# Value sums added by VectorE out of PSUM, both heads' maxima closed together, seven banks in plain rotation

## The chip, the cores and the metric

The kernel runs on one core of one Trainium2 chip. The metric is device time in microseconds, the median of several executions. TensorE (PE, with its weight loads shown as PEld), VectorE (DVE), ScalarE (ACT), GpSimd (POOL) and SyncE (SP, which here only issues transfers) each work through their own list of instructions in order and wait for each other by semaphores. TensorE writes its products into PSUM, which has eight banks of 128 partitions x 512 fp32 numbers; DVE and ACT read them there.

## The reference

The output mixes two branches over the same input x (2048 tokens, 512 features) by a gate for each token:

```python
g = _sigmoid((x * gate_w).sum(-1, keepdims=True))
a = _A_ref(x, A_wqkv, A_wo)
b = _B_ref(x, B_w_gate, B_w_up, B_w_down)
return g * a + (1 - g) * b

# _A_ref: softmax attention, 32 heads of 16, then @ wo
scores = jnp.einsum("bhqd,bhkd->bhqk", q, k) * scale
p = _softmax(scores, axis=-1)
o = jnp.einsum("bhqk,bhkd->bhqd", p, v)

# _B_ref: gated unit with hidden size 1792
h = _sigmoid(x @ w_gate) * (x @ w_up)
return h @ w_down
```

All is fp32. The softmax is taken with the row maximum subtracted, so for each head and query the maximum over 2048 keys has to be known before the exp.

## The kernel before

**Setup (to about 90 us).** The first projections and v are computed, and the maxima of the first queries.

**Main loop.** 16 pairs of heads, 16 steps for each, 256 steps k in all (`NPER`). The two heads of a pair live in the two row halves of TensorE: head b uses partitions 64b and up. One step does five kinds of work, in an order that is written out by hand:

- *Score products* (`st_part`, L638): keys x queries of a pair, 128 keys x 512 queries each, eight a step; ACT turns each into p by an exp (L640). A fifth group of rows of the query tile `QS` carries the negative maximum of that query, so the product is already shifted. In even steps all eight are of head 0 (`t0`), in odd steps of head 1 (`t1`): four for this step and four for the next.
- *Maximum products* (`sm_step`, L298): queries x keys without the shift, eight steps (head 0) or ten (head 1) ahead of their use; DVE reduces each to a maximum per query (L300) in a tile `stat`. They are `m0` and `m1` in the order.
- *Half products* (`dense`, `d0` and `d1`): twelve a step, of half the rows each, into the bank `dn`; they are the remaining q and k projections (L152) and the gated unit's products (L172). When a sum is done, ACT copies it out (`leave`, L573), and POOL combines it further through a list of jobs, `later`, of which `work(n)` runs n.
- *The value product* (`values(k)`, L779) at the end of a step: p times v of four blocks of keys for both heads, 32 weight loads and products with all rows of TensorE, into one bank. Four steps make a sum. ACT copies the first of the four into `sum` and the others into `part` (L784); POOL adds `part` to `sum` (L797) as the first job of `later`, and after the fourth SP stores it (`pv_d`). In the last eight steps (`TAIL`) DVE makes these copies (L786).
- *Closing maxima* (`close_max`): a block is 512 queries of one head. When its sixteen reduces are done, DVE takes the maximum of four (L312), POOL splits it into two parts in the next step (L102, L103), DVE turns it from columns into rows (L322) two steps after the closing, and SP sends it into `QS` by four small transfers (L328). The heads are closed apart: head 1's block two steps ahead of head 0's.

**What sets the order.** The order on each engine is that of the program. `STEADY` names the products of an even and of an odd step for the first 248 steps, `LAST` those of the last eight. `place` gives out banks: seven banks circulate (`seven`), and by `REUSE` a product takes the bank that was given out six, seven or eight places earlier, so 17 places make a step (eight t, eight m, one value product). A product waits until the engine that reads the bank's last content is through with it. `urgent` holds what the next step does at the word `work`.

**After the loop (from about 1490 us)** the hidden layer's down product and the heads' output product run, almost all on TensorE.

Of the kernel before, what the change touches and what calls it, by code (L numbers as in the profile page):

```python
# [25 lines left out]
P = 128  # L26
# [9 lines left out]
FIRST = 16  # L36
# [14 lines left out]
def gated_mix(ctx, tc, x, xc, xmix, wqk, wv, wo, w_gu, w_down, gate_w, out):  # L51
# [214 lines left out]
    square = turns([(mxs[:, i, 40:44].bitcast(F32), mxs[:, i, :40]) for i in range(2)])  # L266
# [18 lines left out]
    def sm_step(j):  # L285
# [5 lines left out]
        def one(b, i):  # L291
            part = (p, qt // 4, b)
            if part not in stat:
                stat[part] = keep.tile([P, 4, 4], F32, name=f"stat{p}_{qt // 4}_{b}", tag="stat", bufs=8)
                count[part] = 0
# [4 lines left out]
            dve.tensor_reduce(stat[part][:, qt % 4, g:g + 1], t, axis=AX.X, op=ALU.max)  # L300
            count[part] += 1
            if count[part] == 16:
                full.append(part)
# [4 lines left out]
    def close_max():  # L308
        part = full.pop(0)
        p, i, b = part  # L310
        m, hl = square()
        dve.tensor_reduce(m, stat.pop(part), axis=AX.X, op=ALU.max)  # L312
        two = hl[:, :8].rearrange("p (t c) -> p t c", c=2)
# [4 lines left out]
        def turned():  # L318
            f = hl.bitcast(F32)
            blocks = bass.AP(f.tensor, f.offset, [f.ap[0], (2, 4), (1, 32)])  # L320
            mt = keep.tile([P, 4, 32], F32, name=f"mt{p}_{i}_{b}", tag="mt", bufs=2)
            dve.transpose(mt, blocks)  # L322

            def send():
                r = 64 * b + 3 * DH
                rows = QS[p % 2][r:r + 2, i * 512:(i + 1) * 512].bitcast(F32).rearrange("a (t g j) -> a g t j", g=4, j=32)
                for g in range(4):
                    sp.dma_start(rows[:, g], mt[32 * g:32 * g + 2])  # L328
# [348 lines left out]
    bank7 = turns(seven)  # L677
# [91 lines left out]
    def values(k):  # L769
# [12 lines left out]
        def copy(e):  # L782
            if k < NPER - TAIL:
                act.activation(e, o, AF.Copy)  # L784
            else:
                dve.tensor_copy(e, o)  # L786

        if part not in sums:
            sums[part] = keep.tile([P, 256], F32, name=f"sum{p}_{c}", tag="sum", bufs=2)
            copy(sums[part])  # L790
        else:
            e = keep.tile([P, 256], F32, name=f"part{k}", tag="part", bufs=2)
            copy(e)
            later.insert(0, lambda s=sums[part]: add(s, e))

        def add(s, e):
            pool.tensor_tensor(s, s, e, ALU.add)  # L797
            if k % 4 == 3:
                sp.dma_start(pv_d[c, p], s)
# [17 lines left out]
    count_given = [0]  # L817

    def place():
        b = given[-REUSE[count_given[0] % len(REUSE)]]  # L820
        count_given[0] += 1
        given.append(b)
        return b
# [32 lines left out]
    for k in range(NPER):  # L856
        n = 2 * k
        if n + FIRST == NSTEP:
            bank = bank7
# [206 lines left out]
```

## Time and profile before

| | |
|---|---|
| median of 3 runs | 1679.14 us (1679.1 to 1679.32) |
| span of the profiled execution (no other time of it is listed) | 1677.7 us |
| TensorE clock granted | 1.000 |
| busy: DVE, ACT, POOL | 1430.2, 1338.9, 1053.4 us |
| L300 reduces out of `sm` and `st` banks | 1124 and 924, 682 ns each |
| L640 exps out of `sm` and `st` banks | 1217 and 831, 625 and 628 ns each |
| L784 copies on ACT | 248, 385 ns each |
| L797 sums on POOL | 192, 737 ns each |
| L322 transposes, L312 closing maxima on DVE | 128 each, 302 and 128 ns |

How to read the rows: in a timeline each row is the start in us, the length, the engine, the line, the operation, what it writes and reads (out<-in, buffer numbers left out), the form, and how many like instructions were merged; in brackets stands the idle time of the engine in front of it and what ended it. Products are pipelined, so that PE seems always busy; PEld, the weight loads, shows better when PE waits. A group's row gives count, busy time in all, and the mean length.

### The profile page before, as it was taken

The page shows a single profiled execution, that of the slowest core. Times are in us where ns is not written, and L with a number is a line of the kernel's source. Part 1 is how long each engine was busy: PE and PEld are TensorE (multiplying, and loading weights), DVE is VectorE, ACT ScalarE, POOL GpSimd, SP SyncE. Part 2 cuts the span into 40 slices and gives each one's busy share as a digit, 9 for nine tenths or more (in the row PEclk, how much of TensorE's full clock was granted, in tenths as well). Part 3 has the DMA queues.
Part 4 walks back from the last instruction along what each step waited for, and adds up shares of the span by engine and source line. Part 5 has one row for each costly group of instructions (what it writes and reads, how often), then busy time and mean ns, then how long its engine had stood idle before and what let it go on. Part 6 is the DMA issues. An engine that isn't in the chain of part 4 may idle for free.

```text
span 1677.7 us, 43606 instructions
## 1 busy us (share of the span) xinstructions
PE 1672.6 (100%) x16594; PEld 1148.7 (68%) x16594; DVE 1430.2 (85%) x2456; ACT 1338.9 (80%) x2680; POOL 1053.4 (63%) x1238
## 2 busy tenths in 40 slices
PE   9999999999999999999999999999999999999999
PEld 7866666666666666666666666666666666678887
DVE  6989998999999999999999999999999999668653
ACT  4188888888888888888888999999999988974421
POOL 1146665368888888776676897777777767752110
PEclk9999999999999999999999999999999999999999
DMA  9624666454444444442347353423343425268860
GB/s 257 133 80 171 176 206 191 136 152 144 118 149 133 127 140 129 126 118 72 94 151 209 121 138 106 118 92 95 102 100 93 110 79 183 70 226 298 276 198 25
DMA packets 131554, 236.68 MB, mean 141 GB/s; under 512 B 19409, under 2 KB 39889, under 8 KB 128337
## 3 DMA queue, kind: packets, MB, share of 16 engines
q1 hardware_dynamic: 131056, 233.37, 47.1%
q8 instruction: 131, 2.15, 0.6%
q14 instruction: 79, 0.64, 0.1%
q10 hardware_dynamic: 288, 0.52, 0.1%
HBM read 155.71 MB, written 77.59 MB: 139 GB/s over the span
## 4 chain that ended last, share of the span: by engine, by line
PE 99%; DVE 0%; ACT 0%; issue 0%; POOL 0%; ACTq 0%
PE dn L172 23%; PE sm L779 22%; PE sm L298 10%; PE st L298 9%; PE st L779 8%; PE dn L152 7%; PE sm L1002 6%; PE sm L638 4%; PE st L139 4%; PE st L638 3%; PE dn L1002 2%; PE st L152 1%; PE st L1002 1%; PE st L87 0%; ACT p L640 0%; DVE stat L300 0%
## 5 line engine op out<-in xcount | busy, mean ns | idle before, releaser
L300 DVE TENSOR_REDUCE stat<-sm 128x1 f32<-128x512 f32 x1124 | 727.9, 682 | 73.7 <-PE sm L298 30.4
L640 ACT ACTIVATE p<-sm 128x512 f32<-128x512 f32 x1217 | 682.2, 625 | 7.5 <-PE sm L638 5.3
L300 DVE TENSOR_REDUCE stat<-st 128x1 f32<-128x512 f32 x924 | 606.7, 682 | 63.2 <-PE sm L638 24.2
L640 ACT ACTIVATE p<-st 128x512 f32<-128x512 f32 x831 | 495.0, 628 | 1.6 <-PE dn L152 0.2
L172 PE MATMUL dn<-xm,mh 64*128 64x512 f32 x1568 | 485.5, 389 | 0.0
L638 PE MATMUL sm<-qs,ks 64*128 64x512 f32 x1217 | 445.1, 403 | 0.0
L298 PE MATMUL sm<-ks,qs 48*128 48x512 f32 x1124 | 420.8, 421 | 0.1
L298 PE MATMUL st<-ks,qs 48*128 48x512 f32 x924 | 368.0, 426 | 0.0
L779 PE MATMUL sm<-p,v 128*17 128x256 f32 x6080 | 365.2, 380 | 0.1
L638 PE MATMUL st<-qs,ks 64*128 64x512 f32 x831 | 324.7, 408 | 0.0
L172 PEld LDWEIGHTS dn<-xm,mh 64*128 64x128 f32 x1568 | 289.5, 185 | 29.3
L172 PE MATMUL dn<-xm,ml 64*128 64x512 f32 x784 | 304.2, 388 | 0.0
L779 PEld LDWEIGHTS sm<-p,v 128*17 128x17 f32 x6080 | 160.4, 97 | 169.4 <-ACT p L640 58.5
L298 PEld LDWEIGHTS sm<-ks,qs 48*128 48x128 f32 x1124 | 199.9, 184 | 87.4 <-DVE stat L300 77.0
L638 PEld LDWEIGHTS sm<-qs,ks 64*128 64x128 f32 x1217 | 219.0, 185 | 16.0 <-issue 2.1
L298 PEld LDWEIGHTS st<-ks,qs 48*128 48x128 f32 x924 | 167.1, 184 | 83.6 <-DVE stat L300 75.5
L797 POOL TENSOR_TENSOR sum<-sum,part 128x256 f32<-128x256 f32 x192 | 141.5, 737 | 77.7 <-ACT part L784 49.5
L423 POOL TENSOR_TENSOR m<-m,m 128x512 f32<-128x512 f32 x140 | 178.1, 1290 | 5.9 <-ACT m L573 3.9
L638 PEld LDWEIGHTS st<-qs,ks 64*128 64x128 f32 x831 | 152.4, 185 | 11.6 <-issue 1.3
L172 PEld LDWEIGHTS dn<-xm,ml 64*128 64x128 f32 x784 | 144.4, 184 | 11.5
L102 POOL CAST mxs<-mxs 128x4 fp32r<-128x4 f32 x128 | 24.1, 188 | 201.2 <-DVE mxs L312 200.8
L125 POOL TENSOR_TENSOR ml<-r,mh 128x512 fp32r<-128x512 f32 x112 | 143.9, 1285 | 7.0
(313 smaller groups left out, 2351.1 us busy)
## 6 DMA issues: line engine op xcount, KB each, us to landing
r<-in_w_gu_dram SPq DMA_DIRECT2D x112, 256.0 KB
gul<-gu_d SPq DMA_DIRECT2D x56, 512.0 KB
gu_d<-m SPq DMA_DIRECT2D x84, 256.0 KB
xm_d<-xm SPq DMA_DIRECT2D x32, 512.0 KB
xm<-xm_d SPq DMA_DIRECT2D x32, 512.0 KB
xm<-in_xmix_dram SPq DMA_DIRECT2D x24, 512.0 KB
qs<-q_d SPq DMA_DIRECT2D x90, 128.0 KB
ks<-k_d SPq DMA_DIRECT2D x90, 128.0 KB
```

The costliest lines, as they stand in the source:

```text
L125: pool.tensor_tensor(l, src, h.bitcast(F32), ALU.subtract)
L139: pe.matmul(o, a, b, start=(i == 0), stop=(i == len(ops) - 1))
L152: mm = pe.matmul(self.o, a[rows], b[rows], start=(self.n == 0), stop=(self.n == 2 * len(self.ops) - 1))
L172: pe.matmul(self.o, a, b, start=(self.n == 0), stop=(self.n == len(self.ops) - 1))
L298: pe.matmul(t, qs[r:r + KM, qt * P:(qt + 1) * P], ks[r:r + KM, g * 512:(g + 1) * 512], start=True, stop=True)
L300: dve.tensor_reduce(stat[part][:, qt % 4, g:g + 1], t, axis=AX.X, op=ALU.max)
L423: pool.tensor_tensor(o, x, y, op)
L638: pe.matmul(o, ks[r:r + KR, (kt + a) * P:(kt + a + 1) * P], qs[r:r + KR, c * 512:(c + 1) * 512], start=True, stop=True)
L640: act.activation(pt[:, a, :], o, AF.Exp, scale=DH ** -0.5)
L779: pe.matmul(o[r:r + VW, :], v[:, 4 * k % 16 + a, h * VW:(h + 1) * VW], pts[b][:, a, 256 * i:256 * i + 256], start=(a == 0), stop=(a == 3))
L797: pool.tensor_tensor(s, s, e, ALU.add)
L1002: pe.matmul(down[t], a, b, start=(f == 0 and m == 0), stop=(f == NF - 2 and m == 5))
```

## The change

It has four parts.

- `values`: DVE does what ACT and POOL did with the value product. The first of four is copied from PSUM to `sum` by DVE, the other three are added to `sum` by DVE straight from PSUM. `part` and POOL's sums are gone; the store goes through `urgent`. `work` runs one job less at the end of three of four steps, since the sum no longer takes a place in the list.
- `close_max`: a `stat` tile holds both heads; it is closed after 32 reduces by one L312, one split and one L322, and SP sends eight transfers, head 1's first.
- Banks: `REUSE` and its start are gone; `place` goes round the seven banks.
- `STEADY`: another order of the same words, `work` among them.

```diff
--- before.py
+++ after.py
@@ -263,7 +263,7 @@
 
     act.activation(g1[:, :1], warm, AF.Exp)
     mxs = keep.tile([P, 2, 64], F32R, name="mxs")
-    square = turns([(mxs[:, i, 40:44].bitcast(F32), mxs[:, i, :40]) for i in range(2)])
+    square = turns([(mxs[:, i, 48:56].bitcast(F32), mxs[:, i, :48]) for i in range(2)])
     pool.memset(mxs.bitcast(F32), 0.0)
     ones = v.rearrange("p t (h c) -> p t h c", c=VW)[:, :, :, DH]
     pool.memset(ones, 1.0)
@@ -289,17 +289,17 @@
         qs, ks = QS[p % 2], KS[p % 2]
 
         def one(b, i):
-            part = (p, qt // 4, b)
+            part = (p, qt // 4)
             if part not in stat:
-                stat[part] = keep.tile([P, 4, 4], F32, name=f"stat{p}_{qt // 4}_{b}", tag="stat", bufs=8)
+                stat[part] = keep.tile([P, 4, 2, 4], F32, name=f"stat{p}_{qt // 4}", tag="stat", bufs=4)
                 count[part] = 0
             r, g = 64 * b, 2 * kh + i
             t = bankm()
             pe.matmul(t, qs[r:r + KM, qt * P:(qt + 1) * P], ks[r:r + KM, g * 512:(g + 1) * 512],
                       start=True, stop=True)
-            dve.tensor_reduce(stat[part][:, qt % 4, g:g + 1], t, axis=AX.X, op=ALU.max)
+            dve.tensor_reduce(stat[part][:, qt % 4, b, g:g + 1], t, axis=AX.X, op=ALU.max)
             count[part] += 1
-            if count[part] == 16:
+            if count[part] == 32:
                 full.append(part)
         return one
 
@@ -307,25 +307,26 @@
 
     def close_max():
         part = full.pop(0)
-        p, i, b = part
+        p, i = part
         m, hl = square()
-        dve.tensor_reduce(m, stat.pop(part), axis=AX.X, op=ALU.max)
-        two = hl[:, :8].rearrange("p (t c) -> p t c", c=2)
+        dve.tensor_reduce(m, stat.pop(part).rearrange("p t b g -> p (t b) g"), axis=AX.X, op=ALU.max)
+        two = hl[:, :16].rearrange("p (u c) -> p u c", c=2)
 
         def halves():
             split(two[:, :, 0], two[:, :, 1], m, pool, pool)
 
         def turned():
             f = hl.bitcast(F32)
-            blocks = bass.AP(f.tensor, f.offset, [f.ap[0], (2, 4), (1, 32)])
-            mt = keep.tile([P, 4, 32], F32, name=f"mt{p}_{i}_{b}", tag="mt", bufs=2)
+            blocks = bass.AP(f.tensor, f.offset, [f.ap[0], (4, 4), (1, 32)])
+            mt = keep.tile([P, 4, 32], F32, name=f"mt{p}_{i}", tag="mt", bufs=2)
             dve.transpose(mt, blocks)
 
             def send():
-                r = 64 * b + 3 * DH
-                rows = QS[p % 2][r:r + 2, i * 512:(i + 1) * 512].bitcast(F32).rearrange("a (t g j) -> a g t j", g=4, j=32)
-                for g in range(4):
-                    sp.dma_start(rows[:, g], mt[32 * g:32 * g + 2])
+                for b in (1, 0):
+                    r = 64 * b + 3 * DH
+                    rows = QS[p % 2][r:r + 2, i * 512:(i + 1) * 512].bitcast(F32).rearrange("a (t g j) -> a g t j", g=4, j=32)
+                    for g in range(4):
+                        sp.dma_start(rows[:, g], mt[32 * g + 2 * b:32 * g + 2 * b + 2])
             return send
         return halves, turned
 
@@ -674,7 +675,6 @@
     for _, turned in closed:
         turned()()
     seven = [maxb[0], maxb[1], banks[2], maxb[2], banks[1], maxb[3], banks[0]]
-    bank7 = turns(seven)
     chunks = [(c, f) for c in range(NC) for f in range(0, NF, 2)]
 
     def hidden_load(c, f):
@@ -779,24 +779,17 @@
                     pe.matmul(o[r:r + VW, :], v[:, 4 * k % 16 + a, h * VW:(h + 1) * VW],
                               pts[b][:, a, 256 * i:256 * i + 256], start=(a == 0), stop=(a == 3))
 
-        def copy(e):
-            if k < NPER - TAIL:
-                act.activation(e, o, AF.Copy)
-            else:
-                dve.tensor_copy(e, o)
-
         if part not in sums:
             sums[part] = keep.tile([P, 256], F32, name=f"sum{p}_{c}", tag="sum", bufs=2)
-            copy(sums[part])
+            dve.tensor_copy(sums[part], o)
         else:
-            e = keep.tile([P, 256], F32, name=f"part{k}", tag="part", bufs=2)
-            copy(e)
-            later.insert(0, lambda s=sums[part]: add(s, e))
-
-        def add(s, e):
-            pool.tensor_tensor(s, s, e, ALU.add)
-            if k % 4 == 3:
-                sp.dma_start(pv_d[c, p], s)
+            dve.tensor_tensor(sums[part], o, sums[part], ALU.add)
+        if k % 4 == 3:
+            store = lambda s=sums[part]: sp.dma_start(pv_d[c, p], s)
+            if k < NPER - 1:
+                urgent.append(store)
+            else:
+                store()
 
     def mx(b):
         for j in range(UPPER if b else FIRST, NSTEP):
@@ -814,13 +807,7 @@
             yield
 
     urgent = []
-    count_given = [0]
-
-    def place():
-        b = given[-REUSE[count_given[0] % len(REUSE)]]
-        count_given[0] += 1
-        given.append(b)
-        return b
+    place = turns(seven)
 
     def emit(order, **parts):
 
@@ -836,14 +823,8 @@
                 if next(parts[word], place) is place:
                     place()
 
-    STEADY = ("m1 t0 t0 d1 d1 m0 t0 d1 d1 m0 m0 d1 d1 t0 work d1 t0 t0 d1 t0 d1 d1 m0 d1 t0 d1 m0 m0 m1",
-              "m0 t1 t1 d0 m1 d0 t1 d0 d0 m1 t1 d0 d0 m1 work d0 t1 d0 m1 t1 d0 t1 d0 t1 d0 d0 m1 m1 m0")
-    REUSE = (8, 7, 6, 8, 7, 7, 7, 6, 8, 7, 7, 7, 7, 6, 8, 7, 7,
-             6, 8, 6, 8, 7, 7, 7, 6, 8, 7, 7, 7, 7, 7, 7, 7, 6)
-    given = [*range(99)]
-    for j in range(20 * len(REUSE)):
-        given.append(given[-REUSE[j % len(REUSE)]])
-    given = [seven[sorted(set(given[-20:])).index(b)] for b in given[-20:]]
+    STEADY = ("t0 m1 t0 d1 d1 m0 d1 t0 m0 d1 d1 t0 t0 d1 work d1 d1 m0 t0 d1 m0 t0 d1 t0 d1 d1 m0 m1 m0",
+              "m0 t1 d0 t1 m1 d0 d0 t1 d0 d0 t1 d0 m1 d0 work m1 t1 d0 t1 m1 d0 t1 d0 t1 d0 m1 d0 m0 m1")
     LAST = ["t0 d1 t0 d1 t0 d1 t0 d1 d1 work t1 t1 t1 t1", "t0 d1 t0 d1 t0 d1 t0 d1 work t1 t1 t1 t1"] * 2 + [
         "t0 t0 t0 t0 work t1 d0 t1 d0 t1 d0 t1 d0 d0", "t0 t0 t0 t0 work t1 d0 t1 d0 t1 d0 t1 d0"] * 2
 
@@ -855,8 +836,6 @@
     ahead_h = []
     for k in range(NPER):
         n = 2 * k
-        if n + FIRST == NSTEP:
-            bank = bank7
         if 320 <= n < 448 and n % 16 == 0:
             logit_load((n - 320) // 8)
         if n % 32 == 0 and n // 32 + 1 < NPAIR:
@@ -890,7 +869,7 @@
             next(ahead_h[-1])
         if n in (308, 312, 316, 320):
             next(ahead_h[(n - 308) // 4])
-        work(3 if isinstance(run, Sum) and k % 2 else 4)
+        work((3 if isinstance(run, Sum) and k % 2 else 4) - bool(k % 4))
         urgent.extend(jobs)
         if 320 <= n < 448:
             t = (n - 320) // 16 * 2
@@ -986,7 +965,7 @@
     heads = {}
     for n, (c, f) in enumerate(chunks):
         if f == 0:
-            down = [bankt() if 4 * c + t != AHEAD else None for t in range(4)] if c else [maxb[3], banks[0], maxb[0], maxb[1]]
+            down = [bankt() if 4 * c + t != AHEAD else None for t in range(4)] if c else [maxb[0], maxb[1], banks[2], maxb[2]]
         if n == 4:
             g = g0[:, AHEAD:AHEAD + 1]
             dve.tensor_scalar(ahead, dn, g, None, op0=ALU.mult)
```

The rows that follow are the engines' lists as the programs give them, from the middle of the loop (steps 130 and 131); `st` and `sm` with a number are the seven banks, `x2` two alike. Lines past L314 of the changed program are shifted by one or more: L639 there is L638 here, and L329 is L328.

TensorE before, from the last rows of the value product of step 129 into the even step 130:

```order
L779 MATMUL sm_72<-p_1_11202,v 17x256 x2
L779 MATMUL sm_72<-p_0_11149,v 17x256 x2
L298 MATMUL sm_70<-ks_102,qs_101 128x512
L638 MATMUL st_65<-qs_101,ks_102 128x512
L638 MATMUL sm_71<-qs_101,ks_102 128x512
L172 MATMUL dn<-xm_2_4373,mh_0_5_1_10933 128x512 x2
L298 MATMUL sm_69<-ks_102,qs_101 128x512
```

The same place now:

```order
L779 MATMUL st_66<-p_1_10801,v 17x256 x2
L779 MATMUL st_66<-p_0_10740,v 17x256 x2
L639 MATMUL sm_72<-qs_101,ks_102 128x512
L298 MATMUL st_65<-ks_102,qs_101 128x512
L639 MATMUL sm_69<-qs_101,ks_102 128x512
L172 MATMUL dn<-xm_2_4231,mh_0_5_1_10543 128x512 x2
L298 MATMUL sm_70<-ks_102,qs_101 128x512
```

In the even step a score product is now the first and the maximum product the second; the odd step begins with a maximum product in both programs.

TensorE before, at the end of the odd step 131, from its sixth score product to the value product:

```order
L638 MATMUL st_66<-qs_101,ks_102 128x512
L172 MATMUL dn<-xm_3_4685,ml_0_5_1_11091 128x512
L638 MATMUL sm_72<-qs_101,ks_102 128x512
L172 MATMUL dn<-xm_3_4685,mh_0_5_1_11090 128x512
L638 MATMUL sm_70<-qs_101,ks_102 128x512
L172 MATMUL dn<-xm_3_4685,mh_0_5_1_11090 128x512
L172 MATMUL dn<-xm_3_4685,ml_0_5_1_11091 128x512
L298 MATMUL sm_71<-ks_102,qs_101 128x512
L298 MATMUL sm_69<-ks_102,qs_101 128x512
L298 MATMUL st_67<-ks_102,qs_101 128x512
L779 MATMUL st_66<-p_1_11358,v 17x256 x2
```

The same place now:

```order
L639 MATMUL sm_71<-qs_101,ks_102 128x512
L298 MATMUL st_66<-ks_102,qs_101 128x512
L172 MATMUL dn<-xm_3_4531,ml_0_5_1_10697 128x512
L639 MATMUL sm_72<-qs_101,ks_102 128x512
L172 MATMUL dn<-xm_3_4531,mh_0_5_1_10696 128x512
L639 MATMUL st_65<-qs_101,ks_102 128x512
L172 MATMUL dn<-xm_3_4531,mh_0_5_1_10696 128x512
L298 MATMUL sm_69<-ks_102,qs_101 128x512
L172 MATMUL dn<-xm_3_4531,ml_0_5_1_10697 128x512
L298 MATMUL sm_70<-ks_102,qs_101 128x512
L298 MATMUL st_67<-ks_102,qs_101 128x512
L779 MATMUL sm_71<-p_1_10955,v 17x256 x2
```

In both the value product takes the bank of the sixth score product of its step (`st_66` before, `sm_71` now), which is seven places back; two maximum products moved ahead of half and score products, and the three at the end are no longer together.

DVE before, where a step ends and the next begins, in one of the steps with a transpose:

```order
L300 TENSOR_REDUCE stat_2_1_10963<-st_67 128x1
L300 TENSOR_REDUCE stat_2_0_11125<-st_66 128x1
L322 STREAM_TRANSPOSE mt_1_0_11246<-mxs 128x128
L312 TENSOR_REDUCE mxs<-stat_2_1_10963 128x4
L300 TENSOR_REDUCE stat_3_1_11279<-sm_70 128x1
```

The same place now:

```order
L300 TENSOR_REDUCE stat_2_10574<-sm_72 128x1
L300 TENSOR_REDUCE stat_2_10574<-sm_70 128x1
L300 TENSOR_REDUCE stat_2_10574<-st_67 128x1
L300 TENSOR_REDUCE stat_2_10574<-sm_71 128x1
L322 STREAM_TRANSPOSE mt_1_10845<-mxs 128x128
L786 TENSOR_TENSOR sum_0_10795<-st_66,sum_0_10795 128x256
L300 TENSOR_REDUCE stat_3_10878<-st_65 128x1
```

Between the last reduce of a step and the first of the next there now stands the sum of the value product (L786; L784 in one step of four, where it is a copy). L322 is there in one step of four, as before in one of two, and L312 is in another step of the four.

## The prediction

> **What bounds the kernel now.** I read the page first, then the timeline of neighbouring steps. A step k is one pass of the main loop: eight score products (L638) with their exps (L640), eight maximum products (L298) with their reduces (L300), twelve half products into dn, then the value product (L779).
>
> ```profile
> span 1677.7 us, 43606 instructions
> PE 1672.6 (100%) x16594; PEld 1148.7 (68%) x16594; DVE 1430.2 (85%) x2456; ACT 1338.9 (80%) x2680; POOL 1053.4 (63%) x1238
> ```
>
> The span is 1.4 us under the runs' median of 1679.14, so what I save in the span I take off the median. The 100% of PE counts pipelined products and tells nothing of its idle time; DVE (85% of the span) and ACT (80%) are both near it, so each could set the step. Which one does is read from one step, and the timeline shows steps like it all through the main loop:
>
> ```profile
> 807.64 1.43 PEld L779 LDWEIGHTS sm<-p,v 128*17 128x17 f32 x32 [0.31 <-ACT p L640]
> 808.11 1.28 DVE L300 TENSOR_REDUCE stat<-sm 128x1 f32<-128x512 f32 x2
> 808.38 0.68 ACT L573 ACTIVATE m<-dn 128x512 f32<-128x512 f32 x1
> 809.50 0.50 PE L298 MATMUL st<-ks,qs 48*128 48x512 f32 x1
> 809.50 0.50 PE L638 MATMUL sm<-qs,ks 64*128 64x512 f32 x1
> 809.69 0.39 ACT L784 ACTIVATE part<-sm 128x256 f32<-128x256 f32 x1 [0.63 <-PE sm L779]
> 810.03 1.29 DVE L300 TENSOR_REDUCE stat<-st 128x1 f32<-128x512 f32 x2 [0.64 <-PE sm L638]
> ...
> 810.56 0.59 ACT L640 ACTIVATE p<-st 128x512 f32<-128x512 f32 x1
> 811.04 1.09 ACT L640 ACTIVATE p<-sm 128x512 f32<-128x512 f32 x2
> 811.99 1.12 ACT L640 ACTIVATE p<-st 128x512 f32<-128x512 f32 x2
> ...
> 813.16 1.43 PEld L779 LDWEIGHTS st<-p,v 128*17 128x17 f32 x32 [0.31 <-ACT p L640]
> ```
>
> The step takes 813.16 - 807.64 = 5.52 us and is a ring of three pieces. From the value product to the first exp, which starts at 810.06 (row further down): 2.42. From the first exp to the sixth: one distance of 0.50 and four of 0.48, 2.41. The sixth exp ends at 811.99 + 1.12 = 813.11, and 0.05 later the value product begins: it takes the bank that this exp has just read. 2.42 + 2.41 + 0.64 + 0.05 = 5.52. ACT is the limit inside the ring, PE waits 0.31 for it. DVE is not: its eighth reduce ends at 808.11 + 1.28 = 809.39 and the next starts at 810.03, when the new maximum product is there: 0.64 idle in each step.
>
> **Is ACT's value copy in the ring?** In time it stands there, at 809.69, ahead of the first exp. But the first exp comes right behind the end of its own product:
>
> ```profile
> 803.98 0.50 PE L298 MATMUL sm<-ks,qs 48*128 48x512 f32 x1
> 803.98 0.49 PE L638 MATMUL st<-qs,ks 64*128 64x512 f32 x1
> 804.55 0.60 ACT L640 ACTIVATE p<-st 128x512 f32<-128x512 f32 x1
> ...
> 810.06 0.60 ACT L640 ACTIVATE p<-sm 128x512 f32<-128x512 f32 x1
> ...
> 1442.08 1.43 PEld L779 LDWEIGHTS sm<-p,v 128*17 128x17 f32 x32 [0.31 <-ACT p L640]
> 1443.94 0.49 PE L638 MATMUL sm<-qs,ks 64*128 64x512 f32 x1
> 1443.94 0.49 PE L152 MATMUL dn<-wd8h,hh 64*128 64x512 f32 x1
> 1444.13 0.39 ACT L784 ACTIVATE part<-sm 128x256 f32<-128x256 f32 x1 [0.61 <-PE sm L779]
> 1444.46 0.60 ACT L640 ACTIVATE p<-sm 128x512 f32<-128x512 f32 x1
> 1447.56 1.43 PEld L779 LDWEIGHTS sm<-p,v 128*17 128x17 f32 x32 [0.51 <-ACT p L640]
> ```
>
> In the even step the score product ends at 804.47 and the exp starts 0.08 later; in the odd one at 810.00 and 0.06 later. In the last rows no maximum product stands ahead of the score product (a half product in the middle of its sum shares the round and nobody waits for it): exp 0.03 after the end, with the same copy ahead of it, and the step is 1447.56 - 1442.08 = 5.48. So 0.03 to 0.05 of the first exp's wait belongs to the maximum product that is issued and reported first. The copy does not hold the exp: it starts 0.37 ahead of it in the odd step, but only 0.33 ahead at 1444.13, so 0.37 isn't needed. It costs something only where it is itself late:
>
> ```profile
> 211.20 1.43 PEld L779 LDWEIGHTS sm<-p,v 128*17 128x17 f32 x32 [0.31 <-ACT p L640]
> 213.53 0.39 ACT L784 ACTIVATE part<-sm 128x256 f32<-128x256 f32 x1 [1.40 <-PE sm L779]
> 213.81 0.59 ACT L640 ACTIVATE p<-sm 128x512 f32<-128x512 f32 x1
> 216.90 1.43 PEld L779 LDWEIGHTS st<-p,v 128*17 128x17 f32 x32 [0.30 <-ACT p L640]
> ...
>   POOL qh L253: 0.9, 1
>   POOL ha L465: 0.6, 1
>   POOL mh L129: 0.6, 1
> ```
>
> Here it came 2.33 behind the value product's start instead of 2.05, waiting for POOL to give back a buffer; the step took 5.70. (The exp follows after 0.28 even.) The last three rows are L784's waits for POOL: three in all.
>
> **The change, part by part.** *Copies and sums.* Off ACT go 248 copies and off POOL 192 sums; neither stands in the ring, except the three late copies: 3 x (5.70 - 5.52) = **-0.5 us**. DVE gets one operation per step, queued between the eighth reduce and the next step's first. Its price before is not shown (PSUM plus SBUF, 128x256); the neighbours are
>
> ```profile
> 24.53 0.69 DVE L241 TENSOR_TENSOR qe<-st,qe 128x512 fp32r<-128x512 f32 x1 [1.74 <-ACT qe L240]
> ...
> 1467.33 0.42 DVE L786 COPY part<-sm 128x256 f32<-128x256 f32 x1 [2.31 <-PE sm L779]
> 1467.67 0.68 DVE L726 SCALAR_TENSOR_TENSOR gul<-gul 128x512 f32<-128x512 f32 x1
> ...
> 803.79 0.30 DVE L322 STREAM_TRANSPOSE mt<-mxs 128x128 f32<-128x128 f32 x1
> 804.02 0.12 DVE L312 TENSOR_REDUCE mxs<-stat 128x4 f32<-128x16 f32 x1
> ```
>
> The sum of a twice as wide product takes 0.69, a reduce of that width 0.68, and the copy of this very width 0.42, with the next operation 0.34 after its start. So the sum holds DVE for 0.34; bounds 0.30 (the transpose) and 0.69 (the wide sum). It can start when the value product is done, at about 809.7, where the copy started; DVE is then free since 809.39, so it is done with the queue at 810.04, and the reduce behind it, which starts at 810.03 today, moves by a hundredth. **0 us**: the 0.64 gap covers it. Behind a late reduce wait the maximum products, then the value product; but that already waits 0.31 for ACT, so a first reduce up to 0.3 late is not seen either. Without that cover each 0.1 us of it costs 25 us over 248 steps.
>
> *Closing both heads at once.* L312 and L322 run 64 times instead of 128, once in four steps each, in the same gap: 809.39 + 0.23 (804.02 - 803.79) is still before 809.7. **0 us**.
>
> *Rotation and order.* By the order of the changed kernel the value product's bank is still that of the sixth exp of its step, in both parities, so the last two pieces of the ring stay. Each parity's order has one place where three products of one row half follow one another out of step with the other half, about 0.23 (one round) of PE each; PE's 0.31 wait covers it. The fourth score product (even) or the third maximum product (odd) now waits for the new sum, done at about 810.1, and is due over 0.5 us later. What changes in the ring is the first piece: even steps now issue the score product ahead of the maximum product, so the exp is reported first; odd steps keep the maximum product ahead. By the rows above 0.03 to 0.05; I take 0.035, near the smaller end. 124 even steps x 0.035 = **-4.3 us**.
>
> *Sends.* Eight transfers follow one transpose instead of four, the second head's first, and that head's go two steps later than today.
>
> ```profile
> L797 POOL TENSOR_TENSOR sum<-sum,part 128x256 f32<-128x256 f32 x192 | 141.5, 737 | 77.7 <-ACT part L784 49.5
> ...
> 804.12 2.65 SPq L328 DMA_DIRECT2D qs<-mt  x4
> ...
> 1002.41 0.30 DVE L322 STREAM_TRANSPOSE mt<-mxs 128x128 f32<-128x128 f32 x1
> ...
> 1006.26 1.43 PEld L779 LDWEIGHTS sm<-p,v 128*17 128x17 f32 x32 [0.31 <-ACT p L640]
> 1007.35 2.78 SPq L328 DMA_DIRECT2D qs<-mt  x4
> ```
>
> Usually SP sends right behind the transpose: issued by 806.77. The first product that reads the second head's row is the fifth of the next step's scores, by the changed order eight rounds behind that step's first, so about 1.96 + 8 x 0.23 = 3.8 after its value product starts: 807.64 + 3.8 = 811.4, 4.6 later. In the slow place of the last three rows SP stood behind waits and other transfers until 1007.35, and four sends were out at 1010.13; the need would be 1006.26 + 3.8 = 1010.1. So a few of the 62 blocks of the main loop come too late, if SP lags as today. POOL, for which SP often waits, loses a sum of 0.74 us in three of four steps (first row), so I take **+0.3 us**, bounds 0 and 5 (the few worst blocks, 1 us each).
>
> In the last eight steps DVE already copies; setup and the final products are untouched: 0. Sum: -0.5 - 4.3 + 0.3 = -4.5, from a span of 1677.7 to 1673.2 and from the median to **1674.6 us**, 0.27% less. 0.2%, 3.4 us, is about what this kernel's runs can tell from no change.
>
> [...] By the rows, reduces that last 0.68 start 0.60 apart (two in 1.28), so the end of one overlaps the next. [...]
>
> **Rivals.**
> - *DVE becomes the bound (slower).* The sum stands among the reduces with its whole duration and makes them do so as well: 5.86 a step, 0.34 more, 248 x 0.34 = +84, 1763 us. It decides as soon as DVE's work exceeds 5.52 a step, which is a sum of over 0.72 beside eight reduces at 0.60, or over 0.49 in the one step of four with a transpose. Against: all rows of that width are at 0.42. 5%.
> - *Late maxima (slower).* The second head's sends overrun their 4.6 us. If the queue in front of SP grows so that the 62 blocks are late by 0.2 us on average, +12, less 4.8: 1687; with only the worst blocks late, +5 and 1679. It decides when the usual margin is gone. For: 1007.35. Against: 804.12. 18%.
> - *No gain in the even steps (the same).* If the exp's extra wait is not the order of reporting but the copy's end or something else that returns, only the 0.5 is left: 1678.6. For: the short step of 5.48 differs in more than the order, since it has a product less. Against: only its first exp is earlier, by about what the step is shorter. 15%.
> - *The copy does hold the exp (faster).* Then odd steps gain some 0.035 as well: 1679.1 - 8.7 - 0.5 + 0.3 = 1670.2. For: exp behind copy in every step. Against: 0.33 and 0.28. 12%.
>
> **How the numbers follow.** The forecast has 50%, with 1672.5 to 1677 its own range; about a sixth of it lies within 0.2%. Faster: 0.42 + 0.11 = 0.53. Within: 0.08 + 0.14 + 0.06 = 0.28. Slower: 0.05 + 0.12 and some of what I don't see, 0.19. The range runs from just below the faster rival, 1669, to the late maxima at 1687; DVE as the bound and later maxima are left out.
>
> **What would show it.** Value products 5.48 and 5.52 apart in turn, with the wait in front of them still for ACT: right. The first exp of an even step 0.03 behind its product, and of an odd one 0.06: right. The sum on DVE at 0.42 with 0.34 to the reduce behind it, and no new wait of PE for it: the zero is right; a wait of PE for DVE in front of the value product would make it wrong. Single steps of 6 us or more where SP's sends stand right before: late maxima. No steps of 5.70 for a late copy.

## The result and the profile after

The changed kernel takes **1727.63 us** (median of 4 runs, 1725.57 to 1729.58) against 1679.12 before: ratio 1.0288, 95% interval 1.0274 to 1.0303. 48.5 us slower, where 4.5 us faster was forecast, and above the range, which ended at 1687. Its profiled execution has the span 1723.8 us, 46.1 more than before. Two executions of the runs below stood far off the others and are left out of the medians: one of b_dve (4037 us) and the profiled one of tick_both (1983 us, at a granted clock of 0.75), so tick_both has a time but no steps.

The head of the page first:

```profile
span 1723.8 us, 43120 instructions
## 1 busy us (share of the span) xinstructions
PE 1694.0 (98%) x16594; PEld 1108.5 (64%) x16594; DVE 1518.0 (88%) x2576; ACT 1248.5 (72%) x2432; POOL 898.8 (52%) x918
```

ACT and POOL got the relief that was meant: 90 and 155 us less than before. DVE took 88 us more. The time was lost elsewhere, and the starts of the value products say where. From the first of them to the 248th it is 1410.0 us, before 1363.3: 46.7 more. This falls into three parts:

| step of the main loop | before | after | in sum |
|---|---|---|---|
| odd (order "m0 t1 ...") | 5.518 | 5.581 | 124 x 0.063 = 7.8 us |
| even (order "t0 m1 ...") | 5.516 | 5.543 | 124 x 0.027 = 3.3 us |
| long steps, what they have above that | 0.5 us in 3 | 36.5 us in 24 | 36.0 us |

**The long steps** come behind the sends of the maxima. A step is here the distance from one value product to the next. The view of one tile's instructions and of who waits for them, for mt (before, no PE stood in this list):

```profile
L329 SPq DMA_DIRECT2D qs<-mt x512: 610/622/873, 62.1 to 1511.8; - x171
...
who waited for it (us, times):
  PE sm L639: 11.9, 7
  PE st L639: 10.5, 5
```

The longest, 10.68 us from the value product of step 70 to that of step 71, in the timeline (rows of DVE, of SP's DMA queue and of PE's weight loads):

```profile
485.98 0.30 DVE L322 STREAM_TRANSPOSE mt<-mxs 128x128 f32<-128x128 f32 x1
...
489.19 0.59 SPq L350 DMA_DIRECT2D xm_d<-xm  x1
...
489.70 1.43 PEld L779 LDWEIGHTS st<-p,v 128*17 128x17 f32 x32 [0.30 <-ACT p L641]
...
492.79 0.33 SPq L340 DMA_DIRECT2D xm<-in_xmix_dram  x1
493.22 5.43 SPq L329 DMA_DIRECT2D qs<-mt  x8
...
497.10 0.29 PEld L639 LDWEIGHTS st<-qs,ks 64*128 64x128 f32 x1 [3.86 <-issue]
```

The transpose is done at 486.3. SP first stores mixed tokens, waits 3 us, loads the next ones, and begins with the maxima only at 493.22. Of eight sends in 5.43 the second head's four are out by 495.9. The product that reads them was ready at 497.10 - 3.86 = 493.24 and starts at 497.10, 1.2 behind the last issue: that is the landing. "issue" is how the view names a wait for which it finds no releaser.

Such a wait also costs after its end. In the table by stretches, the column behind the busy times is PE's granted clock:

```profile
490.00:496.00 6.00, 3.67 (x47) 2.06 (x39) 4.42 (x8) 3.18 (x7) 2.53 (x2) 1.00 0.48 175
496.00:500.00 4.00, 2.87 (x13) 2.29 (x13) 0.69 (x1) 1.88 (x4) 0.00 (x0) 0.58 0.01 1
500.00:504.00 4.00, 4.00 (x37) 1.45 (x36) 2.04 (x5) 0.79 (x2) 1.73 (x4) 0.57 0.12 33
504.00:508.00 4.00, 4.00 (x40) 2.80 (x42) 4.00 (x8) 3.68 (x8) 2.98 (x3) 1.00 0.39 133
```

After 3.86 us of waiting, PE's clock was 0.58 and 0.57 on average over the two middle stretches, so the next step was long too (7.03). The trace's clock records are sharper: 0.50 from 496.63 to 503.45, and in the whole loop 20.5 us at 0.50, in five stretches. Half of that, 10.2 us, is an estimate of the most that the slow clock can have cost; the rest of the 36.5 us is waiting, of which the view of mt finds 22.4.

**The odd steps.** Timeline of one, weight loads and reduces:

```profile
830.18 1.43 PEld L779 LDWEIGHTS sm<-p,v 128*17 128x17 f32 x32 [0.30 <-ACT p L641]
...
832.22 0.42 DVE L784 COPY sum<-sm 128x256 f32<-128x256 f32 x1 [0.24 <-issue]
832.57 0.69 DVE L300 TENSOR_REDUCE stat<-st 128x1 f32<-128x512 f32 x1
833.17 1.50 DVE L300 TENSOR_REDUCE stat<-sm 128x1 f32<-128x512 f32 x2
834.59 0.68 DVE L300 TENSOR_REDUCE stat<-st 128x1 f32<-128x512 f32 x1
...
835.33 0.18 PEld L298 LDWEIGHTS st<-ks,qs 48*128 48x128 f32 x1 [0.31 <-DVE stat L300]
835.75 1.43 PEld L779 LDWEIGHTS st<-p,v 128*17 128x17 f32 x32 [0.24 <-ACT p L641]
```

The sum is where it was expected: 0.42, with 0.35 to the reduce behind it. But two reduces that took 1.28 or 1.29 together now take 1.50: the third starts at 833.17 + 1.50 - 0.69 = 833.98, which is 3.80 behind the value product, in place of 3.59. All later ones are late with it. The fourth ends at 835.27; the last maximum products, which need its bank, start at 835.33, and the value product 0.42 behind them. Its own wait, 0.24 and put down to ACT, hides this: the sixth exp ends at 835.64, so by the ring of before it would have begun at about 835.70. The page's group names what the reduces waited for longest, half products into dn:

```profile
L300 DVE TENSOR_REDUCE stat<-sm 128x1 f32<-128x512 f32 x1201 | 783.2, 684 | 32.4 <-PE dn L172 13.5
```

**The even steps.** Timeline of the next one, first products and first exp:

```profile
837.61 0.49 PE L639 MATMUL sm<-qs,ks 64*128 64x512 f32 x1
837.80 0.42 DVE L786 TENSOR_TENSOR sum<-st,sum 128x256 f32<-128x256 f32 x1
838.17 0.69 DVE L300 TENSOR_REDUCE stat<-st 128x1 f32<-128x512 f32 x1
838.20 0.60 ACT L641 ACTIVATE p<-sm 128x512 f32<-128x512 f32 x1 [1.09 <-PE st L298]
841.30 1.43 PEld L779 LDWEIGHTS sm<-p,v 128*17 128x17 f32 x32 [0.30 <-ACT p L641]
```

The exp starts 0.10 behind the end of its product at 838.10, not 0.03, although the score product is now issued first.

### The profile page after: what moved, and what is told of

It is laid out like the page before. It is cut to its first block, busy times and chain, and to the rows that moved or that the text cites. A ratio compares the mean times of both kernels' runs of the same rounds, so it can differ in the third digit from the quotient of the medians.

```text
span 1723.8 us, 43120 instructions
## 1 busy us (share of the span) xinstructions
PE 1694.0 (98%) x16594; PEld 1108.5 (64%) x16594; DVE 1518.0 (88%) x2576; ACT 1248.5 (72%) x2432; POOL 898.8 (52%) x918
## 4 chain that ended last, share of the span: by engine, by line
PE 93%; DMA 3%; DVE 1%; SPq 1%; ACT 1%; issue 0%; POOL 0%; ACTq 0%; DVEq 0%
PE dn L172 18%; PE sm L779 15%; PE st L779 11%; PE sm L298 8%; PE sm L639 8%; PE sm L981 6%; PE st L298 6%; PE st L639 6%; PE dn L152 6%; PE st L139 4%; PE dn L981 2%; DMA qs<-mt 1%; PE st L152 1%; DMA xm<-xm_d 1%; DVE stat L300 1%; SPq L329 1%
## 5 line engine op out<-in xcount | busy, mean ns | idle before, releaser
L300 DVE TENSOR_REDUCE stat<-sm 128x1 f32<-128x512 f32 x1201 | 783.2, 684 | 32.4 <-PE dn L172 13.5
L641 ACT ACTIVATE p<-sm 128x512 f32<-128x512 f32 x1173 | 662.7, 627 | 171.4 <-PE sm L639 77.2
L300 DVE TENSOR_REDUCE stat<-st 128x1 f32<-128x512 f32 x847 | 564.0, 684 | 19.4 <-PE dn L172 9.2
L172 PE MATMUL dn<-xm,mh 64*128 64x512 f32 x1568 | 505.1, 397 | 0.0
L639 PE MATMUL sm<-qs,ks 64*128 64x512 f32 x1173 | 457.2, 413 | 12.5 <-DMA qs<-mt 11.9
L298 PE MATMUL sm<-ks,qs 48*128 48x512 f32 x1201 | 466.9, 429 | 0.0
L639 PE MATMUL st<-qs,ks 64*128 64x512 f32 x875 | 355.5, 413 | 12.2 <-DMA qs<-mt 10.5
L779 PE MATMUL sm<-p,v 128*17 128x256 f32 x4704 | 284.1, 382 | 0.2
L639 PEld LDWEIGHTS sm<-qs,ks 64*128 64x128 f32 x1173 | 212.5, 186 | 87.2 <-issue 38.8
L779 PE MATMUL st<-p,v 128*17 128x256 f32 x3488 | 212.4, 385 | 0.0
L779 PEld LDWEIGHTS sm<-p,v 128*17 128x17 f32 x4704 | 124.2, 97 | 129.8 <-ACT p L641 42.3
L639 PEld LDWEIGHTS st<-qs,ks 64*128 64x128 f32 x875 | 159.9, 186 | 68.3 <-issue 33.0
L779 PEld LDWEIGHTS st<-p,v 128*17 128x17 f32 x3488 | 92.6, 98 | 97.2 <-ACT p L641 31.4
```

Of the source, the lines that this page charges most:

```text
L172: pe.matmul(self.o, a, b, start=(self.n == 0), stop=(self.n == len(self.ops) - 1))
L298: pe.matmul(t, qs[r:r + KM, qt * P:(qt + 1) * P], ks[r:r + KM, g * 512:(g + 1) * 512], start=True, stop=True)
L300: dve.tensor_reduce(stat[part][:, qt % 4, b, g:g + 1], t, axis=AX.X, op=ALU.max)
L639: pe.matmul(o, ks[r:r + KR, (kt + a) * P:(kt + a + 1) * P], qs[r:r + KR, c * 512:(c + 1) * 512], start=True, stop=True)
L641: act.activation(pt[:, a, :], o, AF.Exp, scale=DH ** -0.5)
L779: pe.matmul(o[r:r + VW, :], v[:, 4 * k % 16 + a, h * VW:(h + 1) * VW], pts[b][:, a, 256 * i:256 * i + 256], start=(a == 0), stop=(a == 3))
```

## The experiments

All runs in one table. "odd" and "even" are the median distances of value products in us, "long" is what single steps have above them (0.18 each where a late copy does it).

| run | us | ratio to before, 95% interval | odd | even | long (steps) |
|---|---|---|---|---|---|
| the change | 1727.63 | 1.0288, 1.0274 to 1.0303 | 5.58 | 5.54 | 36.5 (24) |
| a_split | 1689.84 | 1.0062, 1.0048 to 1.0076 | 5.58 | 5.54 | 0 |
| a_odd | 1724.89 | 1.0277, 1.0263 to 1.0291 | 5.52 | 5.54 | 42.6 (25) |
| b_merge | 1693.79 | 1.0081, 1.0065 to 1.0096 | 5.52 | 5.52 | 15.2 (15) |
| b_dve | 1678.85 | 0.9997, 0.9988 to 1.0006 | 5.52 | 5.52 | 0 |
| b_merge_dve | 1719.92 | 1.0242, 1.0227 to 1.0258 | 5.52 | 5.52 | 38.4 (23) |
| swap_heads | 1817.56 | 1.0831, 1.0809 to 1.0852 | 5.59 | 5.54 | 129 (61) |
| sp_order | 1708.33 | 1.0160, 1.0139 to 1.0181 | 5.58 | 5.54 | 7.8 (6) |
| split_odd | 1682.48 | 1.0012, 0.9994 to 1.0029 | 5.52 | 5.54 | 0 |
| order_alone | 1683.20 | 1.0022, 1.0013 to 1.0031 | 5.52 | 5.54 | 0.6 (3) |
| tick | 1679.74 | 1.0003, 0.9994 to 1.0011 | 5.52 | 5.48 | 0 |
| tick_both | 1675.20 | 0.9977, 0.9967 to 0.9986 | - | - | - |
| tick_wide | 1670.37 | 0.9946, 0.9934 to 0.9959 | 5.48 | 5.48 | 0 |

### Where the long steps come from

**a_split** has the closings of before in the changed kernel:

```diff
-            part = (p, qt // 4)
+            part = (p, qt // 4, b)
-            if count[part] == 32:
+            if count[part] == 16:
...
-                for b in (1, 0):
-                    r = 64 * b + 3 * DH
+                r = 64 * b + 3 * DH
```

> The changed kernel with the two heads' maxima closed, turned and sent apart again, as before; sums, rotation and order stay changed. Theory (late maxima): the 24 long steps, 36.5 us above their neighbours, come from the second head's sends going out two steps later behind SP's queue. Then they vanish: about 1727.6 - 36 = 1691 us, and no step above 5.8. Rival (the sum on VectorE or the rotation makes them): the long steps stay, 1720 or more. In both cases the other steps stay at 5.58 and 5.54.

1689.84, no long step, the others as they were. The joined closings make all 36 us; what is left is 10.5 us above before, the other two parts.

**b_merge** is the reverse, the joined closings alone in the kernel before (the diff's parts in close_max and sm_step and the wider tile mxs, nothing else).

> The kernel before with only the closings of both heads joined. Theory (late maxima): long steps appear without any change to sums, rotation or order. By SP's delays of before behind the transposes of the later head (4.1, 4.9, 4.7, 5.8, 4.9 and some at 3.3 to 3.5) and some 1.3 us lost per us of delay above 3.3, as in the changed kernel, 10 us, and up to 36 if SP's queue shifts as it did there: 1689 to 1715. Rival (joined closings are harmless and the shift of SP comes from the sums): 1679. The other steps stay at 5.52.

1693.79: long steps without any other edit. PE now waits for mt, and SP's queue at the place of the longest step reads

```profile
481.22 0.30 DVE L322 STREAM_TRANSPOSE mt<-mxs 128x128 f32<-128x128 f32 x1
...
481.54 5.46 SPq L329 DMA_DIRECT2D qs<-mt  x8
487.37 0.58 SPq L350 DMA_DIRECT2D xm_d<-xm  x1
```

Here the sends go out at once and the store of mixed tokens comes behind them. So SP's queue stands differently in the changed kernel, and that may be the rest of the 36 us. **b_dve** (sums on VectorE alone) and **b_merge_dve** (both) tell what moved it:

> The kernel before with only the value sums moved to VectorE. Theory: the sum lies in DVE's gap, the steps stay at 5.52 and the three late copies go: 1678.6 us, the same within 0.2%. Rival (the sum itself costs, since DVE has 0.38 less in each step): steps of 5.54 to 5.58, 1685 to 1694.

> The kernel before with closings joined and sums on VectorE; rotation and order as before. The joined closings alone gave 1693.8, with 15 us of long steps; the whole change has 36 us of them. Theory A (the sums' jobs are gone from the list that POOL and SP work off, so SP stands elsewhere when the maxima are ready): some 36 us of long steps, 1715. Theory B (the rest comes from rotation and order): 15 us, 1693.

The sums alone are the same as before within 0.2%: 1678.85, steps of 5.52, and the late copies gone. One step with a transpose and a closing, the fullest gap, of b_dve:

```profile
803.54 0.30 DVE L322 STREAM_TRANSPOSE mt<-mxs 128x128 f32<-128x128 f32 x1
803.76 0.12 DVE L312 TENSOR_REDUCE mxs<-stat 128x4 f32<-128x16 f32 x1
803.94 0.42 DVE L786 TENSOR_TENSOR sum<-sm,sum 128x256 f32<-128x256 f32 x1
804.28 1.28 DVE L300 TENSOR_REDUCE stat<-sm 128x1 f32<-128x512 f32 x2
...
807.39 1.43 PEld L779 LDWEIGHTS sm<-p,v 128*17 128x17 f32 x32 [0.31 <-ACT p L640]
```

Sum 0.42, next reduce 0.34 later, and PE waits 0.31 for ACT as before: the zero of this term is shown. Together with the joined closings, though, the same sums cost 26 us more than the closings alone: theory A. Rotation and order have no part in it. The first send stands 1.35 us behind its transpose on average in b_merge (61 blocks) and 2.58 in b_merge_dve. SP is not among the engines whose order is written by hand (`ORDERED` names PE, ACT, DVE and POOL): with the sums' jobs gone, the build puts the sends behind a store gu_d<-m, which waits for POOL, in 12 blocks, and in none of b_merge. In b_merge_dve the steps behind these 12 hold 16 of the 38 us, and those behind four blocks whose sends follow a load of mixed tokens 11. **sp_order** adds SP to that list in the changed kernel:

```diff
-ORDERED = {E.PE, E.Activation, E.DVE, E.Pool}
+ORDERED = {E.PE, E.Activation, E.DVE, E.Pool, E.SP}
```

> The changed kernel with SyncE in the list of engines whose instructions keep the order in which the code issues them; before, SP's order was left to the scheduler of the build. The other engines' orders are the same. The sends now stand only once, not ten times, right behind a store of mixed tokens and the load that waits for it. Theory (SP's place makes the long steps): the long steps change and become fewer, from 36 us to 15 or less, 1706 or less, and a step is still long only where the fourth send is issued 6.0 or more behind its transpose. Rival (the long steps hang on something else): 36 us as before.

The long steps fell to 7.8 us in the profiled execution, nearly all in one step, where the first send came 5.84 behind its transpose (920.15) and the eight took 7.17:

```profile
920.15 0.30 DVE L322 STREAM_TRANSPOSE mt<-mxs 128x128 f32<-128x128 f32 x1
...
925.99 7.17 SPq L329 DMA_DIRECT2D qs<-mt  x8
```

By its median the gain is 19 us, short of the 21 that the theory gave at least; the profiled execution was the fastest of its four, 1699.5, the other three lay at 1707.5 to 1709.3, so 9 us of the median have no profile. In the profile the part behind the loop is also 2.6 us longer than in the changed kernel (227.2 us from the 248th value product on, against 224.6), which no theory covers. SP's place is shown as the cause, its whole price not.

**swap_heads** asks which of the eight sends is due:

```diff
-                for b in (1, 0):
+                for b in (0, 1):
```

> The changed kernel with the eight sends in the other order: the first head's four ahead of the second's. Theory (the second head's maxima are due some 7.5 us behind the transpose and land over 1 us after they are issued, the first head's have 3.7 us more): the second head's four come 2.7 us later; the long steps began where the fourth send was issued 6.0 behind the transpose, and SP starts 2.3 behind it on average, so most blocks are late, by 2.3 + 5.4 - 6.0 = 1.7 on average: 60 to 110 us more, 1785 to 1840. Rival (the eighth send counts, or the number of sends): no change, 1728.

90 us more, and 44 of 61 blocks late. The due ones are the second head's, and they are due so soon that 2.7 us of delay, four sends, use up the margin of most blocks; the rest are those whose sends follow the transpose at once.

### The odd steps

**a_odd** exchanges two words in the odd order:

```diff
-"m0 t1 d0 t1 m1 d0 d0 t1 d0 d0 t1 d0 m1 d0 work ..."
+"m0 t1 d0 t1 m1 d0 d0 t1 d0 d0 t1 m1 d0 d0 work ..."
```

> The changed kernel with one pair of words exchanged in the odd steps' order: the third maximum product stands ahead of the half product that stood ahead of it. Theory (count in program order): its reduce waits for a count that holds that half product, which runs a round later on the other row half; exchanged, the third reduce starts at 3.59 behind the value product instead of 3.80, and steps go from 5.58 to about 5.52: 124 x 0.06 = 7 us less, 1720. Rival (the plain rotation's banks hold DVE): third reduce at 3.80 or no shorter step, 1727. The long steps stay in both.

```profile
831.13 1.43 PEld L779 LDWEIGHTS sm<-p,v 128*17 128x17 f32 x32 [0.30 <-ACT p L641]
...
834.13 1.31 DVE L300 TENSOR_REDUCE stat<-sm 128x1 f32<-128x512 f32 x2
835.36 0.68 DVE L300 TENSOR_REDUCE stat<-st 128x1 f32<-128x512 f32 x1
...
836.65 1.43 PEld L779 LDWEIGHTS st<-p,v 128*17 128x17 f32 x32 [0.31 <-ACT p L641]
```

The two reduces take 1.31 together, the third at 3.62, the wait for DVE ahead of the value product is gone, the step is 5.52. So it was the half product: m1 ran a round early, on the other row half, and its reduce could not start until the half product that stood ahead of it in the program had ended too. In the odd step of the changed kernel shown above, m1 ends at 833.70, that half product at 833.91, and the reduce starts at 833.98. The programs say the same: the reduce waits for a count of PE's products, and the exchange lowers this count by one. The time fell by only 2.7 of the 7.8 us, less than the executions of either kernel differ among themselves (4.0 and 4.6). In the profiles the long steps grew from 36.5 to 42.6; the sends kept no pace with the shorter steps, the first one standing 2.56 behind its transpose on average in place of 2.33. **split_odd** joins this with the closings apart, where nothing takes it back:

> The changed kernel with closings apart again and the exchanged pair of words in the odd steps' order, both at once. Theory (three separate losses): steps of 5.52 in place of 5.58 as with the exchange alone, 5.54 as before it, no long steps: 1689.8 - 124 x 0.06 = 1682.4. Rival (what the exchange saves comes back elsewhere, as it did in the long steps): 1687 to 1690.

1682.48: 7.4 us less than a_split, so nearly all of the 7.8 is there.

### The even steps

**order_alone** is split_odd with sums on ACT and POOL again, so it is the kernel before with the new rotation and order:

> The kernel before with rotation and order as changed, and the exchanged pair of words in the odd steps: sums on ACT and POOL and closings apart as before. Theory (score product reported first, and the second wait of the exp passed while ACT copies the values): even steps 5.48, odd 5.52: 1679.3 - 124 x 0.036 = 1674.8. Rival (the second wait costs here too): even steps 5.54, 1682. Rival (no gain from the order of reporting): 1679.

The rival came true: 1683.20, even steps 5.54. ACT copies, and the exp still starts 0.09 behind the end of its product at 805.89. The copy does not hold it: it started 0.40 ahead, and before, 0.33 was enough.

```profile
805.39 0.50 PE L638 MATMUL sm<-qs,ks 64*128 64x512 f32 x1
...
805.58 0.38 ACT L783 ACTIVATE part<-st 128x256 f32<-128x256 f32 x1 [0.63 <-PE st L778]
...
805.98 0.60 ACT L640 ACTIVATE p<-sm 128x512 f32<-128x512 f32 x1
```

**tick** takes the second wait away from this exp. In the order of ACT's instructions with their waits, the changed kernel has

```
1215 L574 ACTIVATE m_0_5_1_11000<-dn 128x512 [waits PE_49,Pool_49]
1216 L641 ACTIVATE p_0_11029<-st_66 128x512 [waits PE_49,Activation_49]
1217 L641 ACTIVATE p_0_11029<-st_65 128x512 [waits PE_49]
```

at the start of every even step: the exp waits for PE and for ACT's own earlier exps into the same buffer. Such an exp stood before as the fifth of the odd steps, where ACT is busy and nobody sees it. tick lets an operation of no other use pass that wait, while ACT stands idle:

```diff
+    tick = keep.tile([P, 1], F32, name="tick")
...
+        if k < NPER - TAIL:
+            act.activation(tick, newest[0][:, 3, :1], AF.Copy)
         emit(STEADY[k % 2] if k < NPER - TAIL else LAST[k - NPER], **group)
```

(newest is the tile of exps written last.)

> As split_odd, and at each step's start ACT reads one column of the exps it wrote last, 128x1, so that no first exp has to wait for ACT's own earlier writes beside PE. Theory (second wait): the first exp of the even steps starts 0.03 to 0.04 behind its product instead of 0.10, these steps take 5.48 instead of 5.54: 1682.4 - 124 x 0.06 = 1675. Rival (an ACT that stood idle starts late, whatever it waits for): the exp stays at 0.10 and the time at 1682. Rival (the new small operation is in the way): above 1682.

```profile
801.95 0.50 PE L641 MATMUL sm<-qs,ks 64*128 64x512 f32 x1
...
802.48 1.09 ACT L643 ACTIVATE p<-sm 128x512 f32<-128x512 f32 x2 [0.89 <-PE sm L641]
```

The exp starts 0.03 behind its product though ACT was idle for 0.89, so idleness is not what made it late, and the even steps take 5.48. The main loop gained what was expected, but the time only 2.7: the last stage, after the loop, became 3.8 us longer. All that tick adds to split_odd is a small operation and a tile of 4 bytes in each partition. **tick_both** ("t1 m0" in the odd order too) and **tick_wide** (the same with the tile 512 bytes wide) were to separate this:

> As tick, and in the odd steps' order the first two words exchanged as well, so that the score product stands ahead of the maximum product in both. Theory (reported first): the odd steps go from 5.52 to 5.48 as well: 124 x 0.036 = 4.5 less than tick, 1670.5. Rival (DVE or PE is the next limit in the odd steps): no more than 1 less than tick.

> As tick_both, with the small tile that ACT writes made 512 bytes long in each partition, of which one column is used, in place of 4 bytes. In tick, PE's products followed one another in 231 to 236 ns in the last stage, in place of 227, and the last stage was 3.8 us longer. Theory (tiles behind the small one lie at addresses that are no multiple of 512 bytes or so, and PE reads them more slowly): 227 again and 3.8 to 4.5 us less than tick_both, 1671. Rival (it comes from the shorter steps or from ACT's added instructions): as tick_both, 1675.

tick_both took 4.5 us off tick, as it should if the odd steps win 0.036 each too. tick_wide took another 4.8 off. The group of the last stage's commonest product and one of the others, in tick, and then the commonest in tick_wide:

```profile
L985 PE MATMUL sm<-wd_h,hl 128*128 128x512 f32 x176 | 58.5, 395 | 0.0
...
L985 PE MATMUL sm<-weights,hl 128*128 128x512 f32 x66 | 15.9, 389 | 0.0
```

```profile
L985 PE MATMUL sm<-wd_h,hl 128*128 128x512 f32 x176 | 57.4, 389 | 0.0
```

395 ns against 389 each, and from start to start 231 to 235 against 227. The built programs give the addresses. In tick and tick_both 250 tiles placed behind the small one lie 32 bytes behind a multiple of 512, in tick_wide none of them does. In tick, 552 products of the last stage read one of these: wd_h and wd_l as the streamed operand, oh and ol as the loaded one; all four kinds take 395 or 396 ns. The products of weights and hl, both on multiples of 512, keep their 389 in the same run. Estimated from the distances, 552 x 7 ns = 3.9 us, which is all that this stage lost. **tick_wide, at 1670.37 us, beats both kernels**: 0.54% under before. Its steps:

```profile
791.89 1.43 PEld L781 LDWEIGHTS sm<-p,v 128*17 128x17 f32 x32 [0.30 <-ACT p L643]
797.37 1.43 PEld L781 LDWEIGHTS st<-p,v 128*17 128x17 f32 x32 [0.31 <-ACT p L643]
802.86 1.43 PEld L781 LDWEIGHTS sm<-p,v 128*17 128x17 f32 x32 [0.30 <-ACT p L643]
```

## Why the prediction was wrong, step by step

- *Late copies, -0.5.* Right: ACT copies no value product any more, and b_dve has no step of 5.70.
- *The sum in DVE's gap, 0.* Right, and at the price taken: 0.42, with 0.34 to the next reduce. DVE as the bound through the sum, the rival at 5%, is refuted by b_dve, where the sum stands among reduces 0.60 apart; its 5.86 a step is eight reduces of 0.68 and the sum of 0.42, one behind the other.
- *Closing both heads at once, 0 on DVE.* Right for DVE. Its price was the sends.
- *Sends, +0.3, bounds 0 and 5.* **This is the step that failed, by 36 us.** The mechanism was written down, as a term and as the rival of late maxima, and came true; its size was off for two reasons. "issued by 806.77" and "811.4, 4.6 later" set the issue of the sends against the need, where the landing counts: 1.2 us less margin, as the longest step shows. And "if SP lags as today" did not hold. The lag of SP was taken from before, where the sums still had their jobs on POOL's list; b_merge, with SP's old lag, lost 15 us, and b_merge_dve 38. The note that POOL "loses a sum of 0.74 us", taken as a gain for SP, had the opposite sign. The rival's 1687 priced 62 blocks at 0.2 us each. In truth few blocks were late by much: 24 steps, the longest by 5.1, with a slowed clock behind five of the waits.
- *One round of PE, covered by its wait of 0.31, 0.* Wrong, +7.8 us. The place in the odd order was found, but only PE's time was costed. What it cost was the start of a reduce: 0.21, on DVE, whose later reduces then held the last banks. "DVE is not the limit" held for its sum of work, and not for a hole in the middle of it.
- *Score product reported first, -4.3.* The gain is real: 0.035 a step was taken, and tick and tick_wide show 0.034 between orders (5.517 and 5.483). In the changed kernel it was outweighed by a second wait that came with the same exchange and costs 0.06 on this exp: +3.3 in sum. It could have been read from the waits in the order of instructions; the prediction compared the order only.
- *What would show it.* "Single steps of 6 us or more where SP's sends stand right before: late maxima" was the right thing to look for. "a wait of PE for DVE in front of the value product" is there too, 0.31 ahead of the last maximum products of odd steps, but it doesn't mean what the prediction gave it as: the sum's zero held, and a late reduce makes the wait.

The three parts make 7.8 + 3.3 + 36.0 = 47.1 us, of 46.7 measured in the loop. Open: why sp_order's executions differ by 8 to 10 us, and b_merge's by 6.5; why the build places the sends as it does (only that it does, and what it costs, was shown); and how much of the long steps is clock, beyond the estimate of 10.2 us at most.

## What to carry to other kernels

When several transfers are joined into one later group, price the margin of the earliest one from its landing, not its issue (1.2 us here), and take the lag of its queue from the new order, since removing jobs from another engine may move that queue (here from 1.35 us behind the transpose to 2.58). An engine with enough idle time per step is still the limit if a late start falls in the middle of its run (one of 0.21 us made the odd steps 0.06 longer), so follow each consumer's start and not only sums of work. And compare the waits of the instructions on the critical ring, not only their order: a second wait on the first instruction of the ring was paid in full here, 0.06 us in every even step (5.54 against 5.48).

## What was not expected of the hardware

- **A reader waits for more than its own product.** Two products run at once on the two row halves of PE, and one can start ahead of another that stands before it in the program (833.30 and 833.52 in the odd step shown). Its reduce waits for a count that holds both: it started at 3.80 behind the value product, and at 3.62 with the two exchanged.
- **A second wait cost about 0.06 us** on the first exp of a step: it started 0.10 behind its product with two waits (0.09 in order_alone, where ACT had just copied), 0.03 with one. The same in the fifth exp of a running row cost nothing that the step shows: 5.518 for the odd steps of before, which have it, and 5.516 for the even ones.
- **A long stall of PE slows what follows it.** In the changed kernel the granted clock went to 0.50 for 3.41 us, once 6.83, at waits of 2.38, 2.80, 3.12, 3.18 and 3.86 us; at waits of 2.27 and less it did not. Here a wait is the idle time in front of a weight load. The five slow stretches of the loop begin at 421.53, 448.84, 496.63, 595.61 and 1005.21, the later four 8, 22, 51 and 171 times 3.413 us behind the first. With the loop cut on this grid, each of the five full-speed pieces with 1.90 us or more without a product is followed by a slow one, and none with 1.41 or less. The lengths of the waits, 2.38 and 2.27, divide them as well, so this trace does not tell whether the length decides or the place on the grid.
- **Four bytes cost 4.8 us.** tick_both and tick_wide differ in nothing but the width of one tile, 4 and 512 bytes, and by 4.8 us. Products that read a tile 32 bytes behind a multiple of 512 took 395 or 396 ns in tick, whichever operand it was, in place of the 389 of tick_wide; which multiple it takes was not tried. Why such a tile is read more slowly is not shown.
